# Attention backward loop on one core: result stores and operand loads issued piece by piece over the steps of a head group, and the PE-transposed blocks of dS copied out of PSUM in two pieces of 512 columns instead of four of 256

## The chip, the cores and the metric

The kernel runs on one core of one Trainium2 chip. The metric is device time in microseconds (us) of one execution. Before the change the median of three runs is 2866.06 us (2860.91 to 2873.49).

The core has a matrix engine (PE, with weight loads listed as PEld), a vector engine (DVE), an activation engine (ACT), a general engine (POOL) and a queue engine (SP) that here only issues DMAs. POOL also issues DMAs. All DMAs, whoever issues them, are moved by the same 16 DMA engines.

## The reference

The function is one transformer block with adaptive layer norm and its full backward pass (batch 1, 2048 tokens, width 512, 32 heads of 16, hidden width 1792). Cut to its core:

```python
def _A_ref(x, wqkv, wo):
    qkv = (x @ wqkv).reshape(B, S, 3, H, Dh) -> q, k, v      # H = 32, Dh = 16
    p = softmax(einsum('bhqd,bhkd->bhqk', q, k) * Dh ** -0.5)
    o = einsum('bhqk,bhkd->bhqd', p, v)
    return o.reshape(B, S, D) @ wo
...
h = layernorm(x) * (1 + ca) + sa;  x = x + ga * _A_ref(h, ...)
h = layernorm(x) * (1 + cb) + sb;  x = x + gb * (relu(h @ w1 + b1)**2 @ w2 + b2)
```

The outputs are the block's result and the gradients of x, wqkv, wo, w1, b1, w2, b2, c and w_mod for a given grad_out.

The change touches only the part that computes dQ, dK and dV of the attention. For each head, with E the unnormalised probabilities and dS = E * (dO V^T - delta): dV = E^T dO, dK = dS^T Q, dQ = dS K. The row constants and the 1/sum factors are folded into extra operand rows and pre-scaled operands, so the loop itself has only exponentials, one elementwise product and matmuls.

## The kernel before

The program first projects Q, K, V, runs the attention forward with the MLP forward and backward woven in as filler work (up to about 1300 us), then some weight gradients (the matmuls of line 800 and those before it), and then the backward loop of the attention (lines 813 to 963), which is what the change touches. A last stage turns dQ, dK, dV into the gradients of wqkv, x and the modulation.

**Tiling of the loop.** There are 8 head groups (`hg`) of 4 heads. A head group has 4 key chunks of 512 (`kc4`), each with 16 query tiles of 128 (`qt`), each with two head pairs (`pr`): 128 steps per head group, 1024 in all (`NS`). A step handles 2 heads x 128 queries x 512 keys, that is, a tile of 128 x 1024.

**A step's work.**
- `emit_S` (lines 823 to 833): PE writes the scores of two heads to a PSUM tile (`psS_u`, L829), ACT takes the exponential to SBUF (`E_u`, L833).
- `emit_D` (835 to 854): PE writes dO V^T - delta to a PSUM tile of the same pool (`psD_u`, L841), DVE multiplies it with `E_u` to `dS_u` (L847). `psS_u` and `psD_u` share three PSUM buffers (pool `psu`) in turn, so D of a step takes the buffer that S of the same step leaves when its exponential is done, and S of a step takes the buffer that D three steps earlier leaves when its product is done.
- `emit_V` (L883) and `emit_K` (L891): PE accumulates dV^T and dK^T in one PSUM bank, `accVK`, over the query tiles of a chunk.

**dQ.** It needs dS with keys on the partitions. Two steps (one query tile, four heads) make a `dS_u` tile of 16 blocks of 128 x 128; five such tiles are in use in turn. SP issues a transposing DMA for each (L853) into `dST`. Eight steps (four query tiles) make a group, 128 groups in all. Of the fourth tile of a group only 8 blocks go by DMA; the other 8 are transposed by PE (`emit_T`, L871, two halves of four blocks) into one PSUM bank (`dSt8`), and ACT copies them to `dST` (`emit_C`, L875, four copies of two blocks, 256 columns each). `emit_Q` (L912) then multiplies with K in three parts; ACT copies the result (`dQpart`, L923, or `dQacc`, L920 for the first chunk) and POOL adds it to `dQacc` (L925) or, in the last chunk, to the staged result `dQstage` (L930).

**Order of the work.** The main loop (936 to 963) emits, for step s: the next operand load if one is due, S of step s+1, D of s, V of s-1, K of s-2, and then by j = (s-10) mod 8: the transposes at j = 1 and 2, the copies at j = 1 to 4, the parts of Q at j = 5, 6, 7. All matmuls are chained in this order on PE, and all POOL work in its order on POOL. ACT's and DVE's order is set by the program's scheduler. ACT's order in a group, as it comes out, is: dQpart, two exponentials, copy, exponential, copy, copy, exponential, copy, four exponentials.

**Loads.** `load_one` brings an operand of the next head group: 16 loads of 17 rows x 2048 (68 KB) for `iq`, `ik`, `ido`, `iv`, and three of 512 KB for `sdo`, `sq`, `sk` (L744). They are issued on POOL's queue, one every 5 steps from step 32 of a head group. Each operand has two buffers, used by head groups in turn.

**Stores.** When a head group's dV^T and dK^T are staged in `dVKstage` (L898), `put_rows` (858 to 863) issues its 8 stores of 16 rows x 2048 (64 KB) at once; 4 more follow from `dQstage` about 8 steps later. In the last head group each chunk of 512 columns is stored as soon as it is staged.

**POOL's own order.** A step's number fixes only the place of a load or a store in POOL's order. POOL takes the next one when the one before is issued, unless it has to wait: an addition waits for ACT's copy of dQ, a load for the last reader of its buffer, and every DMA of POOL for the one eight DMAs earlier to have landed (eight semaphores are used in turn). Between two additions POOL therefore issues all that stands there. The first chunk of a head group has no additions, so everything that is put between the last `dQstage` addition (step 17) and the first `dQacc` addition (step 49 or later) stands in one piece. Before the change POOL's order around the start of a head group is: two additions to `dQstage`, each followed by a 512 KB load (`sq`, `sk`); the 8 stores of `dVKstage`; two additions; the 4 stores of `dQstage`; 4 loads of `iq`; then additions with one or two loads behind each.

Of the kernel before, what the change touches and what calls it, by code (L numbers as in the profile page):

```python
# [14 lines left out]
AF = mybir.ActivationFunctionType  # L15
ALU = mybir.AluOpType
AX = mybir.AxisListType
BF = dt.bfloat16
F32 = dt.float32

P = 128
# [3 lines left out]
DH = 16  # L25
HG = 8
# [7 lines left out]
def kernel(  # L34
# [8 lines left out]
    TT = n // P  # L43
    QC = n // 512
# [9 lines left out]
    ACT = nc.scalar  # L54
    POOL = nc.gpsimd
# [44 lines left out]
    qp_st = dram.tile([HG, P, TT, P], BF, name="qp_st")  # L100
    kp_st = dram.tile([HG, P, TT, P], BF, name="kp_st")
    dop_st = dram.tile([HG, P, TT, P], BF, name="dop_st")
# [7 lines left out]
    dT_st = dram.tile([3, D, n], BF, name="dT_st")  # L110
# [28 lines left out]
    with ExitStack() as ph:  # L139
# [5 lines left out]
        for ic in range(DC):  # L145
            pt = psA.tile([P, 8], BF, name="pst", tag="pst")
# [46 lines left out]
    with ExitStack() as ph:  # L193
# [36 lines left out]
        for t in range(TT):  # L230
            for which in range(3):
# [4 lines left out]
                if which < 2:  # L236
                    pad = tokpad[which][t % 2]
                    c0 = DH if which == 0 else 0
# [66 lines left out]
    with ExitStack() as ph:  # L305
# [19 lines left out]
        def chain(key, x):  # L325
            if key in last:
                issue_order(x, last[key])
            last[key] = x
# [405 lines left out]

    loads = {}
    LOADS = [(nm, src, j) for nm, src in (("iq", QtP), ("ik", KtP), ("ido", dOtP), ("iv", VtP)) for j in range(4)]
    LOADS += [("sdo", dop_st, None), ("sq", qp_st, None), ("sk", kp_st, None)]

    def load_one(hg, i):
        nm, src, j = LOADS[i]  # L740
        L = loads.setdefault(hg, {})
        if j is None:
            L[nm] = strm.tile([P, TT, P], BF, name=nm, tag=nm)
            chain("pool", POOL.dma_start(out=L[nm][:], in_=src[hg]))  # L744
        else:
            L[nm] = ops[nm][hg % 2]
            r = 32 * j
            chain("pool", POOL.dma_start(out=L[nm][r:r + DH + 1, :], in_=src[hg][r:r + DH + 1, :]))
# [63 lines left out]
    with ExitStack() as ph:  # L812
# [41 lines left out]
                             in_=dS_q[s // 2].rearrange("q h k -> q (h k)")[:, 0:nb * P], transpose=True)  # L854

        stage = {}

        def put_rows(st, hg, c0, w, parts):
            for t3, off in parts:
                for hq in range(4):  # L860
                    chain("pool", POOL.dma_start(
                        out=dT_st[t3, hg * 64 + hq * DH:hg * 64 + (hq + 1) * DH, c0:c0 + w],
                        in_=st[32 * hq + off:32 * hq + off + DH, c0:c0 + w]))

        def emit_T(g, half):
            if half == 0:
# [5 lines left out]

        def emit_C(g, j):
            pt = acc_t["T", g]
            ACT.activation(dST_t[g][:, 3, 8 + 2 * j:10 + 2 * j, :], pt[:, 2 * j:2 * j + 2, :], AF.Identity)  # L875
            if j == 3:
                del acc_t["T", g]

        def emit_V(s):
# [55 lines left out]

        emit_S(0)
        for s in range(NS + 12):
            r = s % (BLK * QC) - BLK
            if s < NS and r >= 0 and r % 5 == 0 and r // 5 < len(LOADS) and steps[s][0] + 1 < HG:
                load_one(steps[s][0] + 1, r // 5)  # L940
            if s + 1 < NS:
                emit_S(s + 1)
            if s < NS:
                emit_D(s)
            v = s - 1
            if 0 <= v < NS:
                if v % BLK == 0 and v > 0:
                    pass
                elif v % BLK == 1 and v > 1:
                    emit_V(v - 1)  # L950
                    emit_V(v)
                else:
                    emit_V(v)
            if 0 <= s - 2 < NS:
                emit_K(s - 2)
            g, j = divmod(s - GRP - 2, GRP)
            if 0 <= g < NS // GRP:
                if 1 <= j <= 2:
                    emit_T(g, j - 1)
                if 1 <= j <= 4:  # L960
                    emit_C(g, j - 1)
                for kt in ((0,), (1,), (2, 3))[j - 5] if j >= 5 else ():
                    emit_Q(g, kt)

# [153 lines left out]
```

## Time and profile before

| what | time |
|---|---|
| median of three runs | 2866.06 us |
| the profiled execution's own time | 2859.23 us |
| its span | 2857.4 us |
| first exponential of the backward loop to start of the last | 1367.7 to 2722.6 us |
| ACT busy / DVE busy / PE busy in the span | 2265.4 / 1844.6 / 2297.4 us |
| ACT exponentials of the loop, x1024 | 1030.4 us busy |
| DVE products of the loop, x1024 | 1216.8 us busy |
| ACT copies of dSt, x512 | 186.1 us busy, 392 ns mean |
| ACT copies dQpart | 597 ns median |
| 512 KB operand loads, issue to landing | 5.9 to 6.4 us median |
| 64 KB stores of dVKstage, issue to landing | 4.5 us median |
| transposing DMAs, issue to landing | 4.0 us median, 12.5 us at most |

Busy time of a group of instructions counts overlapping ones once. The instructions of ACT and DVE overlap at their ends: an exponential has a mean of 1034 ns, but two in a row start about 0.9 to 1.0 us apart. So a duration is not what an instruction costs in a chain; that is the distance from its start to the start of the next one that waits for nothing else. A row of the timeline has start, length, engine, line, what it writes and reads and the count; in brackets is the idle time of the engine before it and what ended that.

### The profile page before, as it was taken

To read this page: it belongs to the slowest core of one execution; us is meant where nothing else is said; L and a number is where in the kernel's file an instruction comes from. 1 tells how busy PE (TensorE), PEld (TensorE's weight loads), DVE (VectorE), ACT (ScalarE), POOL (GpSimd) and SP (SyncE) were. 2 spreads that over 40 slices of the span, in tenths; PEclk is the share of its full clock that TensorE was granted. 3 is DMA by queue.
4 is the path that set the end of the run, shared out by engine and by line. 5 is a ranking of instruction groups with operands and counts; after the bars stand their busy time and mean duration, and the time that the engine had idled before them with its cause. 6 is when DMAs were issued, how large, how long until landed. Compare 5 with 4: busy or idle time off the path is not lost.

```text
span 2857.4 us, 48379 instructions
## 1 busy us (share of the span) xinstructions
PE 2297.4 (80%) x18261; PEld 782.5 (27%) x18261; DVE 1844.6 (65%) x2376; ACT 2265.4 (79%) x2866; POOL 577.8 (20%) x766
## 2 busy tenths in 40 slices
PE   4888879778877976738888888888888888888868
PEld 2323223222322322314222222222222222222223
DVE  5533344424523442743798998989899898999944
ACT  3699999899989987010798998989899898999912
POOL 7311100410230041053012121111201112121221
PEclk8989969878986987878899999999999999999989
DMA  7931255534543554668699999999999999999985
GB/s 199 223 102 57 75 144 120 135 115 112 130 143 81 120 133 126 155 146 271 141 188 206 190 199 192 188 203 189 197 190 199 196 187 202 184 207 193 181 235 135
DMA packets 1275072, 470.60 MB, mean 165 GB/s; under 512 B 1219635, under 2 KB 1244342, under 8 KB 1273046
## 3 DMA queue, kind: packets, MB, share of 16 engines
q1 hardware_dynamic: 1239268, 357.49, 61.6%
q0 software_dynamic: 32704, 105.82, 12.4%
q10 hardware_dynamic: 2866, 4.20, 0.4%
q8 instruction: 144, 2.36, 0.4%
q14 instruction: 90, 0.74, 0.1%
HBM read 118.49 MB, written 72.56 MB: 67 GB/s over the span
## 4 chain that ended last, share of the span: by engine, by line
PE 16%; ACT 15%; DVE 15%; DMA 7%; issue 6%; SPq 1%; POOL 1%; DVEq 0%; ACTq 0%; POOLq 0%
DVE dS_u L847 13%; ACT E_u L833 12%; PE psD_u L841 4%; PE accVK L883 3%; DMA dST<-dS_u 3%; PE psS_u L829 3%; ACT dST L875 2%; PE dSt L871 2%; PE gb L800 1%; PE accQ L912 1%; DMA tT<-ac 1%; PE jb L1048 1%; DMA h2r<-xn_st 1%; DMA out_dram<-woblk 1%; DMA out_dram<-wqblk 1%
## 5 line engine op out<-in xcount | busy, mean ns | idle before, releaser
L847 DVE TENSOR_TENSOR dS_u<-psD_u,E_u 128x1024 bf16<-128x1024 f32 x1024 | 1216.8, 1220 | 142.8 <-PE psD_u L841 92.1
L833 ACT ACTIVATE E_u<-psS_u 128x1024 bf16<-128x1024 f32 x1024 | 1030.4, 1034 | 80.3 <-PE psS_u L829 56.5
L606 ACT ACTIVATE ET<-sbank 128x1024 bf16<-128x1024 f32 x1024 | 948.6, 1111 | 52.8 <-PE sbank L603 50.9
L841 PE MATMUL psD_u<-iv,ido 32*128 32x512 bf16 x2048 | 412.7, 393 | 170.8 <-ACT E_u L833 155.7
L829 PE MATMUL psS_u<-ik,iq 32*128 32x512 bf16 x2048 | 410.6, 397 | 24.6 <-DVE dS_u L847 18.8
L891 PE MATMUL accVK<-dS_u,sq 128*32 128x512 bf16 x2048 | 415.7, 402 | 0.5 <-DVE dS_u L847 0.5
L883 PE MATMUL accVK<-E_u,sdo 128*32 128x512 bf16 x2048 | 403.8, 403 | 0.0
L603 PE MATMUL sbank<-qt_sb,kt_sb 32*128 32x512 bf16 x2048 | 229.7, 434 | 88.7 <-ACT ET L606 73.3
L613 PE MATMUL oacc<-ET,va 128*32 128x512 bf16 x2048 | 233.7, 445 | 57.3 <-ACT ET L606 54.9
L841 PEld LDWEIGHTS <-ido 32*128 32x128 bf16 x2048 | 164.0, 91 | 357.3 <-issue 355.5
L925 POOL TENSOR_TENSOR dQacc<-dQpart,dQacc 128x512 f32<-128x512 f32 x64 | 80.8, 1262 | 870.9 <-ACT dQpart L923 870.9
L875 ACT ACTIVATE dST<-dSt 128x256 bf16<-128x256 bf16 x512 | 186.1, 392 | 30.5 <-PE dSt L871 30.0
L912 PE MATMUL accQ<-dST,sk 128*32 128x512 bf16 x2048 | 189.9, 392 | 1.2 <-ACT dST L875 1.0
L829 PEld LDWEIGHTS <-iq 32*128 32x128 bf16 x2048 | 102.1, 91 | 320.4 <-issue 294.8
L883 PEld LDWEIGHTS <-sdo 128*32 128x32 bf16 x2048 | 97.4, 93 | 237.8 <-issue 237.8
L603 PEld LDWEIGHTS <-kt_sb 32*128 32x128 bf16 x2048 | 80.8, 93 | 226.1 <-issue 213.0
L613 PEld LDWEIGHTS <-va 128*32 128x32 bf16 x2048 | 66.4, 95 | 257.7 <-issue 257.7
L710 ACT ACTIVATE dwmod_sb<-dmodbc,silucol 128x2048 bf16<-128x2048 bf16 (+1 forms) x8 | 11.9, 1563 | 131.1 <-DVE dmodbc L689 131.1
L275 PE MATMUL xb<-h1T,wpadT 128*128 128x512 bf16 x364 | 99.6, 398 | 15.6 <-DVE pst L574 8.8
L619 DVE COPY ostage<-oacc 128x512 f32<-128x512 f32 x32 | 22.0, 688 | 131.9 <-PE oacc L613 131.9
L871 PE MATMUL dSt<-identb,dS_u 128*128 128x128 bf16 x1024 | 104.4, 226 | 1.2 <-ACT dQpart L923 0.7
L891 PEld LDWEIGHTS <-sq 128*32 128x32 bf16 x2048 | 99.1, 93 | 8.6 <-issue 8.5
(232 smaller groups left out, 2346.4 us busy)
## 6 DMA issues: line engine op xcount, KB each, us to landing
wbig<-in_B_w_dram POOLq DMA_DIRECT2D x8, 1792.0 KB, 9.4
kt_sb<-KtP SPq DMA_DIRECT2D x24, 512.0 KB, 3.7
va<-va_st SPq DMA_DIRECT2D x32, 336.0 KB, 4.3
dST<-dS_u SPq DMA_TRANSPOSE x512, 4.0
wbig<-w2T_st POOLq DMA_DIRECT2D x4, 1792.0 KB, 13.1
wbig<-w1T_st POOLq DMA_DIRECT2D x4, 1792.0 KB, 8.6
dztok_st<-tokh POOLq DMA_DIRECT2D x8, 896.0 KB, 4.8
dzq<-dztok_st SPq DMA_DIRECT2D x4, 1792.0 KB, 26.4
```

The lines of the kernel that those rows point to most:

```text
L603: pe(PE.matmul(pair_ps[hq // 2][:, hq % 2, :], kt_sb[r:r + 32, kt * P:(kt + 1) * P], qt_sb[r:r + 32, :], start=True, stop=True, tile_posit ...
L606: ACT.activation(ET_t[u][:, 2 * pair:2 * pair + 2, :], pair_ps[pair][:], AF.Exp, scale=SCALE)
L613: pe(PE.matmul(oacc[32 * hq:32 * hq + 32, :], lhsT, ET_t[u][:, hq, :], start=(kt == 0), stop=(kt == TT - 1), tile_position=(0, 32 * hq), s ...
L829: pe(PE.matmul(ps[:, hi, :], L["iq"][r:r + 32, qt * P:(qt + 1) * P], L["ik"][r:r + 32, kc4 * 512:(kc4 + 1) * 512], start=True, stop=True, ...
L833: ACT.activation(E_t[s][:], ps[:], AF.Exp, scale=SCALE)
L841: pe(PE.matmul(ps[:, hi, :], L["ido"][r:r + 32, qt * P:(qt + 1) * P], L["iv"][r:r + 32, kc4 * 512:(kc4 + 1) * 512], start=True, stop=True, ...
L847: DVE.tensor_tensor(dS_t[s], ps[:], E_t[s][:], ALU.mult)
L871: pe(PE.transpose(pt[:, j, :], src[:, (8 + j) * P:(9 + j) * P], identb[:]))
L875: ACT.activation(dST_t[g][:, 3, 8 + 2 * j:10 + 2 * j, :], pt[:, 2 * j:2 * j + 2, :], AF.Identity)
L883: pe(PE.matmul(accVK[r:r + 32, :], loads[hg]["sdo"][:, qt, r:r + 32], E_t[s][:, hi, :], start=(qt == 0), stop=False, tile_position=(0, r), ...
L891: pe(PE.matmul(accVK[r:r + 32, :], loads[hg]["sq"][:, qt, r:r + 32], dS_t[s][:, hi, :], start=False, stop=(qt == TT - 1), tile_position=(0 ...
L912: pe(PE.matmul(accQ[r:r + 32, :], L["sk"][:, kc4 * 4 + kt, r:r + 32], dST_t[g][:, :, hq * 4 + kt, :], start=(kt == 0), stop=(kt == 3), til ...
```

## The change

Three things change in the backward loop; PE's, DVE's and SP's instructions and their order stay as they are.

- The three 512 KB loads are each cut into four of 128 KB (128 rows x 512 instead of 128 x 2048). With the 16 others that makes 28 loads per head group, issued one every 3 steps from step 22 (to step 103) instead of 19, one every 5 steps from step 32 (to step 122).
- The stores of a head group are put on a list and issued one at a time, at every fourth step, from step 5 of the next head group (the 8 of dVKstage) to step 49 (the 4 of dQstage). In the last head group everything on the list is issued at once, as before. POOL's order around the start of a head group becomes: three additions to `dQstage`, 2 stores of `dVKstage`, the fourth addition, then 20 DMAs with nothing between them (the other 6 stores of `dVKstage`, the 4 of `dQstage`, and 10 loads: 4 `iq`, 4 `ik`, 2 `ido`), then additions with two or three loads behind each.
- The PE-transposed blocks are copied by ACT in two pieces of 512 columns, at j = 2 and 3, instead of four of 256 at j = 1 to 4. ACT's order in a group becomes: dQpart, three exponentials, copy, exponential, copy, four exponentials.

```diff
-    LOADS += [("sdo", dop_st, None), ("sq", qp_st, None), ("sk", kp_st, None)]
+    LOADS += [(nm, src, 4 + j) for nm, src in (("sdo", dop_st), ("sq", qp_st), ("sk", kp_st)) for j in range(4)]
...
-        if j is None:
-            L[nm] = strm.tile([P, TT, P], BF, name=nm, tag=nm)
-            chain("pool", POOL.dma_start(out=L[nm][:], in_=src[hg]))
+        if j >= 4:
+            if j == 4:
+                L[nm] = strm.tile([P, TT, P], BF, name=nm, tag=nm)
+            ts = slice((j - 4) * TT // 4, (j - 3) * TT // 4)
+            chain("pool", POOL.dma_start(out=L[nm][:, ts, :], in_=src[hg][:, ts, :]))
...
+        rows = []
+
+        def put_row():
+            st, hg, c0, w, t3, off, hq = rows.pop(0)
+            chain("pool", POOL.dma_start(
+                out=dT_st[t3, hg * 64 + hq * DH:hg * 64 + (hq + 1) * DH, c0:c0 + w],
+                in_=st[32 * hq + off:32 * hq + off + DH, c0:c0 + w]))
 
         def put_rows(st, hg, c0, w, parts):
             for t3, off in parts:
                 for hq in range(4):
-                    chain("pool", POOL.dma_start(
-                        out=dT_st[t3, hg * 64 + hq * DH:hg * 64 + (hq + 1) * DH, c0:c0 + w],
-                        in_=st[32 * hq + off:32 * hq + off + DH, c0:c0 + w]))
+                    rows.append((st, hg, c0, w, t3, off, hq))
+            while hg == HG - 1 and rows:
+                put_row()
...
-            ACT.activation(dST_t[g][:, 3, 8 + 2 * j:10 + 2 * j, :], pt[:, 2 * j:2 * j + 2, :], AF.Identity)
-            if j == 3:
+            ACT.activation(dST_t[g][:, 3, 8 + 4 * j:12 + 4 * j, :], pt[:, 4 * j:4 * j + 4, :], AF.Identity)
+            if j == 1:
...
-            r = s % (BLK * QC) - BLK
-            if s < NS and r >= 0 and r % 5 == 0 and r // 5 < len(LOADS) and steps[s][0] + 1 < HG:
-                load_one(steps[s][0] + 1, r // 5)
+            r = s % (BLK * QC) - 22
+            if s < NS and r >= 0 and r % 3 == 0 and r // 3 < len(LOADS) and steps[s][0] + 1 < HG:
+                load_one(steps[s][0] + 1, r // 3)
+            if rows and s % 4 == 1:
+                put_row()
...
-                if 1 <= j <= 4:
-                    emit_C(g, j - 1)
+                if 2 <= j <= 3:
+                    emit_C(g, j - 2)
```

## The prediction

> **What bounds the kernel now.** I read the page first (shares and slices), then the spans of each stage, the waits inside the backward loop, and then the timeline of one undisturbed group, engine by engine, because the shares do not settle it:
>
> ```profile
> L833 ACT ACTIVATE E_u<-psS_u x1024: 1016/1024/1072, 1367.7 to 2722.6; 128x1024 bf16<-128x1024 f32 x171
> ...
> 1537.00:1707.00 170.00, 146.02 (x1424) 45.53 (x1420) 152.80 (x129) 152.62 (x213) 30.24 (x43) 0.97 1.03 198
> ```
>
> The first line (the tile view of E_u) puts the loop between 1367.7 and 2722.6: 1354.9 us for 1023 steps. The second (busy time by stretch; PE, PEld, DVE, ACT, POOL, then granted clock, DMA share, GB/s) is one head group: DVE 152.80 and ACT 152.62 of 170, PE 146.02. Nothing is full. So the loop runs on a chain that crosses engines. One group on ACT:
>
> ```profile
> 1645.81 0.60 ACT L923 ACTIVATE dQpart<-accQ 128x512 f32<-128x512 f32 x1 [0.35 <-PE accQ L912]
> 1646.30 1.94 ACT L833 ACTIVATE E_u<-psS_u 128x1024 bf16<-128x1024 f32 x2
> 1648.46 0.38 ACT L875 ACTIVATE dST<-dSt 128x256 bf16<-128x256 bf16 x1 [0.22 <-PE dSt L871]
> 1648.79 1.02 ACT L833 ACTIVATE E_u<-psS_u 128x1024 bf16<-128x1024 f32 x1
> 1649.71 0.66 ACT L875 ACTIVATE dST<-dSt 128x256 bf16<-128x256 bf16 x2
> 1650.23 1.04 ACT L833 ACTIVATE E_u<-psS_u 128x1024 bf16<-128x1024 f32 x1
> 1651.14 0.42 ACT L875 ACTIVATE dST<-dSt 128x256 bf16<-128x256 bf16 x1
> 1651.40 2.04 ACT L833 ACTIVATE E_u<-psS_u 128x1024 bf16<-128x1024 f32 x2
> 1653.82 1.99 ACT L833 ACTIVATE E_u<-psS_u 128x1024 bf16<-128x1024 f32 x2 [0.39 <-PE psS_u L829]
> 1656.16 0.60 ACT L923 ACTIVATE dQpart<-accQ 128x512 f32<-128x512 f32 x1 [0.35 <-PE accQ L912]
> ```
>
> and the part of PE's that matters:
>
> ```profile
> 1647.37 0.39 PE L841 MATMUL psD_u<-iv,ido 32*128 32x512 bf16 x2 [0.66 <-ACT E_u L833]
> ...
> 1648.03 0.40 PE L871 MATMUL dSt<-identb,dS_u 128*128 128x128 bf16 x4
> 1648.36 0.39 PE L829 MATMUL psS_u<-ik,iq 32*128 32x512 bf16 x2
> ...
> 1653.39 0.39 PE L829 MATMUL psS_u<-ik,iq 32*128 32x512 bf16 x2
> ```
>
> From dQpart to dQpart a group takes 10.35 us. Undisturbed, 1023 steps would take 1023 x 10.35 / 8 = 1323.5; the loop loses 1354.9 - 1323.5 = 31.4 us to stalls. They sit where the 512 KB loads and the stores are:
>
> ```profile
> DVE dS_u L847 <- DMA dST<-dS_u: 19.9, 13, 4.2
> ```
>
> ```profile
> 1700.43 0.56 POOL L744 DMA_DIRECT2D sk<-kp_st  x1
> 1709.34 3.86 POOL L861 DMA_DIRECT2D dT_st<-dVKstage  x8 [8.35 <-ACT dVKstage L898]
> ...
> 1721.53 1.95 POOL L861 DMA_DIRECT2D dT_st<-dQstage  x4 [0.30 <-POOL dQstage L930]
> 1723.47 1.99 POOL L748 DMA_DIRECT2D iq<-QtP  x4
> ```
>
> ```profile
> 1718.57 6.99 DVE L847 TENSOR_TENSOR dS_u<-psD_u,E_u 128x1024 bf16<-128x1024 f32 x6 [1.20 <-DMA dST<-dS_u]
> ...
> 1730.42 4.72 DVE L847 TENSOR_TENSOR dS_u<-psD_u,E_u 128x1024 bf16<-128x1024 f32 x4 [2.20 <-DMA dST<-dS_u]
> ```
>
> ```profile
> 1730.10:1743.80 13.70, 11.93 (x90) 3.34 (x90) 11.50 (x10) 9.77 (x13) 0.00 (x0) 0.63 1.04 201
> ```
>
> DVE waits for a dS_u buffer whose transposing DMA is late (13 times, 19.9 us), and after such a wait the granted clock is 0.63 and the group takes 13.70 instead of 10.35.
>
> **Part 1, the copies.** Removed per group: four copies of 256 columns. Added: two of 512. The first row to look at is the exponential at 1648.79. It starts 0.43 after its S at 1648.36; the one at 1653.82, which waits for PE by the profile, also starts 0.43 after its S (1653.39). So it is PE that sets 1648.79: the chain is exponential end, D at 1647.37, transposes at 1648.03, S at 1648.36. The copy at 1648.46 fills a hole, and taking it out gains nothing. Then ACT runs without a pause to 1651.40: exponential, two copies (1649.71 to 1650.23, 0.52), exponential (0.91), copy (1651.14 to 1651.40, 0.26). That stretch holds three old copies, 0.78 us, and will hold both new ones.
>
> What one new copy takes in it no row shows. From below: the start-to-start of a 256 copy (0.26) and of a 1024 exponential (0.91) give 0.65/768 = 0.85 ns a column, so 512 columns take 0.26 + 0.22 = 0.48. Nearest row: dQpart, 512 columns, 1645.81 to 1646.30, 0.49. From above: its whole length 0.60, if nothing overlapped. I take 0.48: 2 x 0.48 - 0.78 = **+0.18 us a group** (upper end +0.42). The exponential at 1651.40 starts 0.18 later, and D, V, Q and S at 1653.39 follow it in PE's order, so the group ends 0.18 later. Some 15 of 128 groups are disturbed by stalls and would hide it; 113 x 0.18 = **+20 us** (0.165 at the least, +19; with 0.42, +47). A gain is not excluded by this alone; it is the second rival.
>
> One page reads the same rows otherwise. ACT's page share in the loop equals DVE's, and the Trainium skill ("Perfetto Trace Analysis", Optimizing Scalar/DVE Operations) says that a Scalar operation pays about 51 ns of access on PSUM and that grouping helps if the engine is saturated; two operations fewer would by it be -0.10 a group, -13 us over 128. The trace agrees on the size (0.26 less 0.22 for the columns is 0.04) and not on the condition: ACT stands idle before 1648.46, 1653.82 and 1656.16.
>
> The transposes' halves (1648.43 and some 1649.4) end 1.3 us and more before the new copies' places, and the shared PSUM bank is read out by about 1651.7, before Q needs it at 1653.07: no new wait. PE, DVE and SP keep their orders.
>
> **Part 2, stores and loads.** What can go is the 31.4. What is the new pattern? The three 512 KB loads become 128 KB ones, two or three behind each addition, 10 us apart: 0.3 MB per group where sq and sk brought 0.5 MB each. They are finished by step 103, so the last three groups of a head group carry none; before, sk lies right ahead of the stores. I take those stalls as gone. But POOL is not held to the steps: behind the last dQstage addition (1719.96 in the trace) 20 DMAs of 64 or 68 KB stand in one piece where 8 stood (1721.53 and 1723.47). At 0.49 us an issue and at most eight in flight (landing 4.5 us in the median) they take 10 to 15 us and bring 1.3 MB. Before, 2.1 MB fell into the 41 us from sq to iq. So one burst stays, longer than each of the old ones but with nothing ahead of it. How late does it make the transposes? The old burst of 8 stores (3.86 us) moved one transpose's landing from 4.0 to about 7.0 us; a dS_u tile may be late by four tiles of 2.6 us, 10.4 us from issue, before DVE stalls. A burst 2 to 3 times as long adds 6 to 9 us: 10 to 13 us, at the edge. I put 1.5 to 2 us of stall, clock drop included, at each of 7 boundaries, 12 us. So 31 - 12 = **-19 us**. Ends: all gone, -31; the burst as bad as all before, 0, or, with 20 DMAs for 8, another 10 us on top.
>
> The other queues: 9 more DMA issues per head group and 9 ahead of the loop, 72 in all x 0.56 us = 40 us of POOL. It is covered by POOL's waiting for dQpart (870.9 us at L925); a dQ addition can be late by 3 x 0.56 = 1.7 us and its buffer is needed two groups, 20 us, later. Loads start 10 steps earlier, and the last reader of their buffer is at step 9, ahead of 22. SP issues what it did. In the last head group 4 leftover stores join the first 8 (2 us on POOL, no reader until after the loop). The tail's stores come as before.
>
> **Sum.** Against the profiled execution: 2859.2 + 20 - 19 = 2860. It was faster than all three timed runs (2860.91 to 2873.49); the median is 6.8 above it, and I carry half: 2860 + 3.4, say **2863**. No change, then, by the bound of 0.5% (14 us), about what a measurement of this kernel can tell from none.
>
> **Rivals.**
> - *Forecast: the copies cost what the stores return*, 2863. Its own range is 2852 to 2878. Chance 0.50.
> - *The burst takes the place of the old stalls.* 20 DMAs in one piece, eight in flight throughout, hold the transposes up beyond the 10.4 us. For it: two bursts of 8 with 8 us between them already gave 1.20 and 2.20 us of waiting and a clock of 0.63. Against: nothing precedes it now. From a stall of 4.5 us a boundary on (7 x 4.5 = 31) nothing is returned: 2866 + 20 = 2886, slower; with 10 more, 2896. Chance 0.25.
> - *ACT is the bound after all*, and less ACT time is a shorter group: copies' start-to-start was 0.33 + 0.52 + 0.26 = 1.11, becomes 0.96, -0.15 x 128 = -19, with stalls -19: 2863 - 20 - 19 = 2824. For it: ACT is as busy as DVE. Against: the 0.43 above. Chance 0.07. (The page named above would have it; its own figure, -13, gives 2830.)
> - *All stalls go*, as the diff has it: 2859.2 + 19 - 31 = 2847, and since slow runs then lose their excess too I add nothing. Chance 0.18.
>
> **Numbers.** Faster by over 0.5% is below 2851.7: ACT's 0.07, two thirds of the last (0.12), a little of the forecast: 0.21. Slower is above 2880.4: most of the second, 0.24. The same: 0.55. The range leaves out the ACT case and the upper part of the burst: 2842 to 2888.
>
> **What would show it.** Copies: groups of 10.5 instead of 10.35 between dQparts; ACT's waits for psS_u (56.5 us) up by some 60, as the hole at 1648.24 is empty; none for dSt. If groups are 10.2, ACT was the bound. Stalls: DVE's waits for dST's transposes below 10 us and no clock of 0.63 between head groups; if they remain, they should sit 15 to 35 us behind a head group's start, at POOL's 20 DMAs in one piece. A new copy of other than 0.60 us, or a burst that POOL does not issue in one piece, would make me wrong.

## The result, and the profile after

The change takes 2882.65 us in the median (2872.67 to 2891.29 over 20 runs), the kernel before, on the same chips, 2868.93 (2860.91 to 2880.82): a ratio of 1.0035, 95% interval 1.0023 to 1.0048, slower by 0.35%. The forecast was 2863, range 2842 to 2888, and "the same" within 0.5%. The time lies in the range and in the bound of 0.5%. But the forecast stood 0.2% under this median of the kernel before (0.1% under the 2866.06 known then), and the measurement 0.35% above it: the small difference has the other sign.

The profiled execution of the change took 2879.92 us (span 2878.1), 20.7 more than that of before. That is more than the 13.7 between the medians: the profiled execution of before lay 9.7 under its median, that of the change 2.7. So the following shows where time goes, and exaggerates the loss by some 7 us. In the tile view of the exponentials (shortest, middle and longest duration in ns, then first and last start):

```profile
L835 ACT ACTIVATE E_u<-psS_u x1024: 1017/1025/1068, 1363.2 to 2747.1; 128x1024 bf16<-128x1024 f32 x171
```

The backward loop now lasts 2747.1 - 1363.2 = 1383.9 us instead of 1354.9: +29.0. It began 4.5 us earlier and 3.8 us are gained behind it; the loop's start lies between 1363 and 1376 in the runs below, whatever the kernel, so these two say nothing about the change. The busy time of the loop by stretch (stretch, length, then PE, PEld, DVE, ACT and POOL in us, granted clock, DMA share, GB/s), before and after:

```profile
1367.70:2722.60 1354.90, 1163.75 (x11202) 362.81 (x11201) 1214.33 (x1022) 1215.21 (x1689) 237.90 (x339) 0.96 1.00 192
```

```profile
1363.20:2747.10 1383.90, 1169.42 (x11203) 356.14 (x11202) 1219.39 (x1022) 1182.06 (x1435) 269.56 (x396) 0.95 0.96 188
```

ACT has 33 us less to do and the loop takes 29 us more. Three readings divide the 29.

**The undisturbed group.** ACT's timeline of one group after the change (start, us, engine, operation, how many in a row, and in brackets the idle time before with what ended it), and the S matmuls of PE that belong to it:

```profile
1594.85 0.60 ACT L929 ACTIVATE dQacc<-accQ 128x512 f32<-128x512 f32 x1 [0.40 <-PE accQ L921]
1595.35 1.93 ACT L835 ACTIVATE E_u<-psS_u 128x1024 bf16<-128x1024 f32 x2
1597.83 1.02 ACT L835 ACTIVATE E_u<-psS_u 128x1024 bf16<-128x1024 f32 x1 [0.55 <-PE psD_u L843]
1598.75 0.59 ACT L884 ACTIVATE dST<-dSt 128x512 bf16<-128x512 bf16 x1
1599.22 1.03 ACT L835 ACTIVATE E_u<-psS_u 128x1024 bf16<-128x1024 f32 x1
1600.13 0.62 ACT L884 ACTIVATE dST<-dSt 128x512 bf16<-128x512 bf16 x1
1600.61 1.97 ACT L835 ACTIVATE E_u<-psS_u 128x1024 bf16<-128x1024 f32 x2
```

```profile
1597.40 0.39 PE L831 MATMUL psS_u<-ik,iq 32*128 32x512 bf16 x2
...
1602.58 0.39 PE L831 MATMUL psS_u<-ik,iq 32*128 32x512 bf16 x2
```

The exponential at 1597.83 still starts 0.43 behind its S at 1597.40. The place where the first small copy stood is now 0.55 us of idle ACT. The two copies take 1598.75 to 1599.22 and 1600.13 to 1600.61, 0.47 and 0.48 start to start, and what follows them on ACT starts that much later. In the median a group takes 10.495 us instead of 10.355: 0.14 x 128 = 17.9 us.

**The half-clock windows.** In a group at full clock (first line) and in one with a half-clock window (second line), and in the window itself (third):

```profile
1474.69:1485.19 10.50, 8.74 (x92) 2.72 (x88) 9.30 (x9) 9.12 (x11) 2.83 (x4) 1.00 1.06 214
1463.24:1474.69 11.45, 9.93 (x92) 2.83 (x88) 9.92 (x9) 9.23 (x11) 2.30 (x3) 0.85 0.97 213
1470.70:1474.10 3.40, 3.40 (x32) 0.76 (x28) 2.83 (x3) 2.05 (x3) 0.00 (x0) 0.50 1.02 229
```

For 3.4 us the clock is 0.50, PE is busy throughout, and the group takes 11.45 instead of 10.50: 0.95 us. Such windows begin always at the same place, 7.3 to 7.7 us after the start of a group's copy of accQ (dQpart or dQacc), 14 times in the loop. Two of the 14 belong to stalls between head groups (1566.27, and 2088.51, which lasts 13.65 us). The other 12 are single windows inside a head group, at least 14 us from any wait of DVE for a DMA. Before the change there were 4, at 7.35 to 7.4. Eight more at 0.95 are 7.6 us.

**The stalls between head groups.** What is left of the loop is 1383.9 - 1342.0 (1023 steps at 10.495 / 8) - 12 x 0.95 = 30.5 us; before it was 1354.9 - 1324.1 - 4 x 0.95 = 27.0. So in this pair of executions the stalls, from which the prediction took 19 us, are all still there. The waits of DVE and POOL (waiting tile, what it waited for, then us in total, times, longest):

```profile
DVE dS_u L849 <- DMA dST<-dS_u: 15.8, 7, 4.7
...
POOL dT_st L863 <- DMA iq<-QtP: 12.8, 5, 3.2
```

Seven waits of DVE, at five of the 7 boundaries between head groups, have taken the place of 13 (19.9 us before). At a sixth boundary PE waits 1.6 us for a transposing DMA instead, and the last has no stall. POOL's timeline at one boundary, and DVE's behind it:

```profile
1548.88 1.25 POOL L939 TENSOR_TENSOR dQstage<-dQpart,dQacc 128x512 bf16<-128x512 f32 x1 [8.29 <-ACT dQpart L932]
1550.09 1.49 POOL L863 DMA_DIRECT2D dT_st<-dVKstage  x3
1551.56 1.01 POOL L750 DMA_DIRECT2D iq<-QtP  x2
...
1559.87 0.50 POOL L863 DMA_DIRECT2D dT_st<-dQstage  x1 [3.18 <-DMA iq<-QtP]
...
1565.39 0.50 POOL L863 DMA_DIRECT2D dT_st<-dQstage  x1
1605.97 1.26 POOL L934 TENSOR_TENSOR dQacc<-dQpart,dQacc 128x512 f32<-128x512 f32 x1 [40.09 <-ACT dQpart L932]
```

```profile
1565.07 2.36 DVE L849 TENSOR_TENSOR dS_u<-psD_u,E_u 128x1024 bf16<-128x1024 f32 x2 [0.67 <-DMA dST<-dS_u]
1570.19 4.63 DVE L849 TENSOR_TENSOR dS_u<-psD_u,E_u 128x1024 bf16<-128x1024 f32 x4 [2.76 <-ACT E_u L835]
```

```profile
1570.30:1584.40 14.10, 12.53 (x90) 3.39 (x90) 11.83 (x10) 10.12 (x13) 0.00 (x0) 0.64 1.00 199
```

From 1550.09 to 1565.89 POOL issues the 20 DMAs that the program puts at steps 13 to 49, and then waits 40 us for its next addition. DVE waits for a transposing DMA at the end of the burst and once more, for ACT, behind it, and the next group (last fence, by stretch) runs at a clock of 0.64 and takes 14.10 us.

### The profile page after: what moved, and what is told of

Same layout as the page of the kernel before. It is cut to its first block, busy times and chain, and to the rows that moved or that the text cites. A ratio compares the mean times of both kernels' runs of the same rounds, so it can differ in the third digit from the quotient of the medians.

```text
span 2878.1 us, 48099 instructions
## 1 busy us (share of the span) xinstructions
PE 2287.2 (79%) x18153; PEld 775.5 (27%) x18261; DVE 1851.3 (64%) x2376; ACT 2232.9 (78%) x2610; POOL 618.0 (21%) x838
## 4 chain that ended last, share of the span: by engine, by line
PE 16%; ACT 15%; DVE 12%; issue 9%; DMA 7%; SPq 1%; POOL 0%; ACTq 0%; DVEq 0%; another core or an unknown queue 0%; POOLq 0%
ACT E_u L835 12%; DVE dS_u L849 10%; PE psD_u L843 4%; PE accVK L892 3%; PE psS_u L831 3%; DMA dST<-dS_u 3%; ACT dST L884 3%; PE dSt L880 2%; PE accQ L921 1%; PE gb L802 1%; DMA tT<-ac 1%; PE jb L1059 1%; DMA h2r<-xn_st 1%; DMA out_dram<-woblk 1%; DMA out_dram<-wqblk 1%
## 5 line engine op out<-in xcount | busy, mean ns | idle before, releaser
L835 ACT ACTIVATE E_u<-psS_u 128x1024 bf16<-128x1024 f32 x1024 | 1015.2, 1033 | 166.0 <-PE psD_u L843 153.5
L843 PEld LDWEIGHTS <-ido 32*128 32x128 bf16 x2048 | 158.0, 91 | 383.0 <-issue 380.9
L921 PE MATMUL accQ<-dST,sk 128*32 128x512 bf16 x2048 | 196.2, 403 | 4.9 <-DMA dST<-dS_u 3.6
L884 ACT ACTIVATE dST<-dSt 128x512 bf16<-128x512 bf16 x256 | 154.3, 603 | 1.2 <-PE dSt L880 0.7
```

Source lines behind the costliest of these rows:

```text
L835: ACT.activation(E_t[s][:], ps[:], AF.Exp, scale=SCALE)
L843: pe(PE.matmul(ps[:, hi, :], L["ido"][r:r + 32, qt * P:(qt + 1) * P], L["iv"][r:r + 32, kc4 * 512:(kc4 + 1) * 512], start=True, stop=True, ...
L884: ACT.activation(dST_t[g][:, 3, 8 + 4 * j:12 + 4 * j, :], pt[:, 4 * j:4 * j + 4, :], AF.Identity)
L921: pe(PE.matmul(accQ[r:r + 32, :], L["sk"][:, kc4 * 4 + kt, r:r + 32], dST_t[g][:, :, hq * 4 + kt, :], start=(kt == 0), stop=(kt == 3), til ...
```

## The experiments

The theory with which I began: the copies cost what they were said to cost, and the burst makes the stalls, since POOL, which nothing holds back, carries out 40 us of the program at once. Rivals: the stalls are due to the amount of data and not to its bunching; ACT's time is what counts; the windows of half clock are chance. "At that place" below means half-clock windows that begin 6.9 to 7.7 us after the start of the group's copy of accQ. Windows and groups (the median length) are counted in the one profiled execution of each kernel. Ratios are to the kernel before, with 95% intervals; the kernel before was measured again beside each batch of runs (medians 2865.72 to 2873.30), so runs of different batches are compared by their ratios. The added matmuls write a tile that the following S overwrites, and the added POOL copy writes a tile that nobody reads.

### One half of the change at a time

The kernel before with the two copies alone:

```diff
-            ACT.activation(dST_t[g][:, 3, 8 + 2 * j:10 + 2 * j, :], pt[:, 2 * j:2 * j + 2, :], AF.Identity)
-            if j == 3:
+            ACT.activation(dST_t[g][:, 3, 8 + 4 * j:12 + 4 * j, :], pt[:, 4 * j:4 * j + 4, :], AF.Identity)
+            if j == 1:
...
-                if 1 <= j <= 4:
-                    emit_C(g, j - 1)
+                if 2 <= j <= 3:
+                    emit_C(g, j - 2)
```

> Only the copies are changed: two of 512 columns at j = 2 and 3 instead of four of 256; loads and stores as before. Theory A (the copies are the loss: each group is longer because both copies stand on ACT's chain, and the longer stretch in which PE mostly waits lets the clock gate take away half the clock for one 3.41 us window more often): groups of 10.50 us instead of 10.35 (+18 us over 128), single half-clock windows inside a head group up from about 4 to about 13 (0.95 us each, +8), stalls between head groups as before (about 26 us): 20 to 28 us slower than before, ratio 1.007 to 1.010. Theory B (the new pattern of loads and stores is the loss, the copies are neutral as in a stretch with slack): groups of 10.35, within 4 us of before.

Measured: 2894.04, ratio 1.0070 (1.0039 to 1.0100); group 10.497, 12 windows at that place.

The change with the four copies of 256 columns kept (the same diff backwards):

> Only the loads and stores are changed; the four copies of 256 columns stay. Theory A: groups of 10.35 us and few half-clock windows as before; POOL issues 20 DMAs in one piece behind the last addition to dQstage, and the stall moves from the end of a head group to its second and third group without getting smaller: 25 to 30 us of it, within 6 us of before. Theory B: 15 to 25 us slower than before. Theory C (the stores and loads are spread as the step numbers say): stalls nearly gone, 20 to 28 us faster.

Measured: 2862.14, ratio 0.9970 (0.9952 to 0.9987); group 10.355, 6 windows. DVE's waits for the transposing DMAs, with the copies alone and with the spreading alone:

```profile
DVE dS_u L847 <- DMA dST<-dS_u: 27.8, 14, 5.8
```

```profile
DVE dS_u L849 <- DMA dST<-dS_u: 16.5, 7, 5.2
```

What follows: the parts add up (+0.70 - 0.30 = +0.40%, measured +0.35%). The copies cost 20 us (0.70% of 2868.93; by the interval 11 to 29). The spreading returns 9 (0.30%; 4 to 14) and not 19. The 7 waits belong to the spreading.

### POOL held to the steps

A copy of one column that needs a fresh `dQacc` makes POOL wait in each of the first four groups of a head group, so that what the program puts behind it isn't issued before. It is added to the spreading alone:

```diff
+        pace = stg.tile([P, 1], F32, name="pace", bufs=1)
...
+                    chain("pool", POOL.tensor_copy(pace[:, 0:1], dQacc[:, qc * 512:qc * 512 + 1]))
```

> As the run with loads and stores alone, plus one small POOL copy per group of the first key chunk (128x1, reads what ACT has just written to dQacc), so that POOL waits for every group and issues 4 or 5 DMAs per 10 us there instead of 20 in one piece. Theory A (the burst makes the stall): stalls between head groups fall from 26 to 29 us to under 8, no half-clock windows longer than 3.41 us between head groups: 18 to 25 us faster than before. Rival (the amount of bytes in the first 40 us of a head group makes it, not the burst): as the run with loads and stores alone.

Measured: 2833.33, ratio 0.9875 (0.9850 to 0.9900). POOL's timeline behind the same additions:

```profile
1565.07 0.18 POOL L931 COPY pace<-dQacc 128x1 f32<-128x1 f32 x1 [8.06 <-ACT dQacc L930]
1565.29 0.48 POOL L864 DMA_DIRECT2D dT_st<-dVKstage  x1
1565.78 1.01 POOL L750 DMA_DIRECT2D iq<-QtP  x2
1566.78 0.50 POOL L864 DMA_DIRECT2D dT_st<-dVKstage  x1
1575.41 0.18 POOL L931 COPY pace<-dQacc 128x1 f32<-128x1 f32 x1 [8.13 <-ACT dQacc L930]
```

Four DMAs, then 8 us of waiting: no wait of DVE for a transposing DMA is left anywhere in the loop, which by stretch is

```profile
1372.10:2702.00 1329.90, 1145.27 (x11202) 357.74 (x11201) 1214.72 (x1022) 1211.66 (x1689) 279.71 (x438) 0.98 1.00 196
```

The loads and stores are those of the spreading alone, in number and size, only later. So the bunching makes the stalls, not the data: 2862.14 - 2833.33 = 29 us. Against the kernel before it is 1.25%, 36 us, more than the 18 to 25 that were expected. The same line added to the whole change:

> The whole change, plus the small POOL copy per group that makes POOL wait in the first key chunk. Theory A: the burst's stalls (29 us in the profile of the change) go to under 4 us, the copies' cost stays (groups 10.50 us, 12 to 14 half-clock windows at 0.95 us): 22 to 29 us faster than the change, 26 us slower than the paced run with the old copies: 2854 to 2862 us, 8 to 15 us faster than before. Rival (the copies' loss is bound up with the burst): 2833 to 2840 us.

Measured: 2854.54, ratio 0.9960 (0.9946 to 0.9974); group 10.494, 12 windows, no wait of DVE for a DMA. By the ratios the pace is worth 0.75% here, 21 us (0.95%, 27 us, on the spreading alone), and the copies cost 0.85%, 24 us, against the paced spreading (0.70% without the pace). Within the intervals the two halves are independent.

### The copies put into the hole

If the copies cost what they cost by their place, they should gain when they stand where ACT waits for PE. The kernel before with transposes and copies one step earlier, the copies at j = 1 and 2:

```diff
-                if 1 <= j <= 2:
-                    emit_T(g, j - 1)
-                if 1 <= j <= 4:
-                    emit_C(g, j - 1)
+                if 0 <= j <= 1:
+                    emit_T(g, j)
+                if 1 <= j <= 2:
+                    emit_C(g, j - 1)
```

> Two copies of 512 columns, but the PE transposes are put one step earlier (j = 0 and 1) and the copies too (j = 1 and 2), so that the first copy falls into ACT's idle time before the third exponential; loads and stores as before. Theory A (a group is a chain over PE and ACT, and only what is on it counts): between the third and the fifth exponential stands one copy of 0.48 us instead of 0.78 us of copies: groups of 10.0 to 10.1 us, 30 to 42 us faster than before less what half-clock windows take or give. Rival (ACT's or DVE's total work sets the group): DVE's 9.5 us are unchanged and ACT's work falls by 0.15, so 10.2 at best.

Measured: 2879.79, ratio 1.0039 (1.0012 to 1.0067). The undisturbed group is 10.18, shorter than the 10.355 of before by 0.175 (the expectation said 10.0 to 10.1), and yet the loop does not gain. Two stretches of it, the loop and one run of seven groups:

```profile
1369.20:2730.50 1361.30, 1208.41 (x11200) 379.14 (x11200) 1203.23 (x1022) 1207.77 (x1435) 238.75 (x339) 0.94 1.00 191
...
1402.60:1475.00 72.40, 66.52 (x564) 18.56 (x564) 61.31 (x51) 59.49 (x72) 6.18 (x8) 0.79 0.80 165
```

DVE's waits for DMAs are down to 2.1 us, but the granted clock is 0.94 over the loop, and 0.79 over seven groups on end: 30 stretches at half clock in the whole loop, one in each group for a while. Half-clock stretches last whole multiples of 3.41 us, and in each run that has them their starts lie on one grid of that step. Three steps are 10.24, close to this group's 10.18, so once a window of the clock falls on the wrong place, it falls close to it again in the next groups. With the windows, a shorter group is no faster kernel. The place of the copies is worth 0.3 us a group (10.495 to 10.18), and something else is taking the clock.

With the paced spreading added:

> Paced loads and stores together with the early transposes and the two early copies. Groups of 10.18 us are close to three clock windows (3 x 3.41 = 10.24), so the group drifts slowly past the windows and half-clock windows come in rows of five and more, as in the run with early copies alone: 20 to 30 of them at 0.9 us, no stall between head groups. Theory A: 2835 to 2845 us, no faster than the paced run with the old copies, although each undisturbed group is 0.17 us shorter. Rival (the rows of half-clock windows were set off by the stalls at the loads and stores): 2810 to 2818 us.

Measured: 2846.43 (2824.66 to 2860.7), ratio 0.9915 (0.9886 to 0.9945); group 10.18, 35 half-clock stretches in the loop (12 of them at that place), loop 1351.0 at a clock of 0.93. That is just above the 2835 to 2845 expected, and far from the rival's 2810 to 2818: the rows of windows come without any stall, and the kernel is slower than the paced spreading with the old copies, whose group is longer.

### What takes the clock inside a group

The windows begin at one place, so they follow on one stretch: with windows of 3.41 us, the stretch from 4.0 us to 7.4 us after the start of the copy of accQ, which is steps j = 3 to 5, where ACT has both copies and PE waits for ACT. PE waits in it twice, 0.36 and 0.37 us; in the 3.41 us before the window at 1470.70 it is busy for 2.68. The first attempt was to keep PE busy there, by S written twice at j = 3 and 4:

```diff
-            for hi in range(2):
+            for hi in (0, 1, 0, 1) if (s - 11) % GRP in (3, 4) else (0, 1):
```

> The run with the copies alone, and PE does the S matmuls of two steps a group twice (j = 3 and 4, same result into the same PSUM tile), in time in which it waits for ACT. Theory A (single half-clock windows come because PE does too little in the stretch of the two copies): single windows of 3.41 us inside head groups fall from 14 to at most 4, groups stay at 10.50 us, 8 to 12 us faster than the run with the copies alone. Rival (the windows come from something else, an instruction fetch or the DMAs): as many windows as before, and the same time or a little more.

Measured, on the copies alone: 2898.44, ratio 1.0117 (1.0092 to 1.0142); 16 windows at that place, 7.19 to 7.41, and four more at 8.4 to 8.5. At most 4 were expected, and the refutation is not conclusive: the order on ACT had changed as well, and the two copies stood next to each other.

> The run with paced loads and stores and the four old copies, with the same two S matmuls done twice. Theory A: the 5 single half-clock windows of the paced run go, 4 to 5 us faster than it (2828 to 2830 us). Rival (the filling costs PE time on the chain): the groups grow above 10.35 us and it is slower than the paced run.

Measured, on the paced spreading: 2833.74, ratio 0.9882 (0.9863 to 0.9902), the same as without, where 4 to 5 us were expected; 4 windows instead of 5, here too with copies moved together.

> As the run before it, with the two S matmuls done twice. Theory A (too little PE work in the stretch is what takes the clock away): hardly any half-clock windows, groups of 10.18 us throughout: 128 x 0.17 = 22 us below the paced run with old copies and its 5 windows: 2805 to 2815 us. Rival: no better than without the filling.

Measured, on the early copies: 2815.48, ratio 0.9813 (0.9790 to 0.9835), the fastest kernel of all, 31 us less than without the fill; 2 windows in the loop instead of 35:

```profile
1371.00:2722.00 1351.00, 1211.42 (x11208) 377.68 (x11207) 1205.18 (x1023) 1208.57 (x1435) 279.88 (x438) 0.93 0.99 193
```

```profile
1363.10:2680.20 1317.10, 1226.86 (x11712) 384.68 (x11712) 1194.83 (x1022) 1211.65 (x1435) 279.84 (x438) 0.99 1.03 198
```

The first line is the loop with early copies and pace, the second the same with S twice: 510 matmuls more on PE, 34 us less. But the group is 10.22 here, nearer to three windows and drifting otherwise, so the fill and the drift are not told apart by this run alone. The fill at three steps (j = 3, 4, 5):

> Paced loads and stores, early transposes and copies, S twice at j = 3, 4 and 5. The run with j = 3 and 4 had 2 half-clock windows left inside the loop. Theory A: nothing left to gain there, the third extra pair stands on PE ahead of a D that no longer waits: 0 to 5 us slower than 2815. Rival (more PE work still helps): below 2810.

Measured: 2828.79, ratio 0.9862 (0.9841 to 0.9884), 2 windows; but 30 groups took 10.68, and by the ratios the kernel is 14 us slower than with two fills, where 0 to 5 were expected. That the third fill stands on PE's chain is my reading, and no run shows it.

Back to the copies alone, filled where ACT's order stays as it was (j = 4 and 5, `in (4, 5)` in the same line):

> The copies alone, and S done twice at j = 4 and 5 instead of 3 and 4. In the run with j = 3 and 4 the scheduler also put ACT's two copies next to each other, so it did not tell the causes apart; here ACT's order is that of the run with the copies alone. The half-clock windows there begin 7.4 to 7.6 us behind a dQpart, that is, they follow the 3.41 us from 4.0 on, in which PE does only the steps j = 3 to 5; both extra pairs fall into it. Theory A (too little PE work in these 3.41 us): the windows at 7.4 to 7.6 us, 14 in the run with the copies alone, fall to at most 3 and the groups stay within 0.1 us of 10.50: 8 to 12 us faster than that run. Rival (they are not due to PE's work there): about as many, and the same time.

Measured: 2881.93, ratio 1.0056 (1.0039 to 1.0073); 10 windows, now at 7.09 to 7.28. At most 3 were expected, so that PE's busy time sets it is refuted in this form. S uses 32 rows of weights. So the last form of the theory was that it is not the time that counts but how much of the array is used: one matmul with 128 x 128 weights over 512 columns ahead of S at j = 4 and 5:

```diff
+            for hi in range(1 if (s - 11) % GRP in (4, 5) else 0):
+                pe(PE.matmul(ps[:, hi, :], identb[:], L["ik"][:, kc4 * 512:(kc4 + 1) * 512], start=True, stop=True))
```

> The copies alone, and ahead of the S matmuls at j = 4 and 5 one matmul of 128 x 128 weights by 512 columns into the same PSUM tile, which S then overwrites (the result does not change). S done twice there used a quarter of PE's rows and took the windows from 14 to 10 and from 7.45 to 7.2 us behind dQpart. Theory A (the clock gate counts PE's work in these 3.41 us): a matmul over the whole array counts for more, so at most 4 windows of 3.41 us inside head groups, 6 to 10 us faster than the copies alone. Rival (it does not count PE's work): 10 or more windows.

Measured: 2873.32, ratio 1.0002 (0.9986 to 1.0018), by the ratios 0.68% or 19.5 us less than the copies alone (6 to 10 were expected), and **no** window at that place. Six are left, all behind stalls. PE's timeline at the place:

```profile
1487.80 0.39 PE L843 MATMUL psD_u<-iv,ido 32*128 32x512 bf16 x2
...
1488.45 0.39 PE L828 MATMUL psS_u<-ik,identb 128*128 128x512 bf16 x1
1488.77 0.39 PE L831 MATMUL psS_u<-ik,iq 32*128 32x512 bf16 x2
1489.20 0.39 PE L843 MATMUL psD_u<-iv,ido 32*128 32x512 bf16 x2
```

```profile
1368.90:2757.30 1388.40, 1168.38 (x11202) 356.92 (x11201) 1218.80 (x1022) 1182.86 (x1435) 237.88 (x339) 0.95 0.97 188
```

```profile
1373.30:2735.90 1362.60, 1243.37 (x11457) 386.56 (x11456) 1216.11 (x1022) 1206.33 (x1434) 237.84 (x339) 0.98 0.99 191
```

The added matmul at 1488.45 stands in the 0.36 us for which PE waited anyway. Second and third fence: the loop with the copies alone, and with the two added matmuls. 255 matmuls more, the group in the median as long as before (10.50, though 26 groups take 10.62), and the clock up from 0.95 to 0.98. Twelve windows at 0.95 us are 11 us of the gain; for the rest, the stretches at half clock behind the stalls are shorter too (6.83 us at most, where up to 13.65 were). Twice as many (two at each place):

> The same with two such matmuls at each of the two places (0.43 us of PE, more than the 0.36 us that PE waits there). Theory A: no windows of 3.41 us inside head groups; groups up to 0.15 us longer than 10.50, which takes the gain back: 0 to 10 us faster than the copies alone. Rival: as many windows as with one, and 10 to 20 us slower for the longer groups.

Measured: 2883.85, ratio 1.0049 (1.0028 to 1.0070); no window at that place either, but 28 groups take 10.84: two no longer fit into the wait. And on the early copies with pace, one at j = 3 and 4:

> Paced loads and stores, early transposes and copies, and one full-array matmul ahead of S at j = 3 and 4, where PE waits 0.48 and 0.36 us in the run with early copies. Theory A: no half-clock windows inside head groups, groups of 10.18 to 10.22 us: 2808 to 2815 us, as with S done twice there (2815) or a little better, about 55 us faster than before. Rival (the 10.18 us groups were only lucky against the clock windows when S was done twice): windows come back in rows and it takes 2830 us or more.

Measured: 2822.62, ratio 0.9854 (0.9832 to 0.9875); no window, loop clock 1.00, group 10.327:

```profile
1366.20:2690.00 1323.80, 1241.94 (x11462) 387.29 (x11461) 1201.83 (x1022) 1219.02 (x1435) 279.84 (x438) 1.00 1.02 197
```

The group is far from 10.22, so it is not the drift of the filled version alone that frees a kernel of windows. But the time is above the 2808 to 2815 expected, for the group grows by 0.15 us, and that is paid in each. Without the fill PE waits 0.48 and 0.36 us there, so the matmuls have room; why the group grows even so stays open.

**The array in use, in all traces.** The sixteen traces hold more than these pairs of runs. Take every step of the 3.41 us grid that ran at full clock, from 45 us behind the first exponential of the loop to 10 us before the last, 5797 in all, and add up the matmuls in it: each counts by the part of the 128 x 128 array that its weights cover and by its columns, so that the added matmul of `copies_full45` counts 1 and one S matmul (32 rows) 0.25. Of the 5554 steps with a sum of 6.0 or more, none was followed by half clock; of the 145 with less than 5.6, 142 were; between the two, 56 of 98. PE's busy time does not divide them so: it reached 2.99 us in steps that were followed by half clock, and was under 3.0 in 2586 that were not.

In undisturbed groups the sum is lowest in a stretch that ends 6.6 to 7.2 us behind the copy of accQ: 4.8 before the change, 4.6 with the copies alone, 5.6 with S twice at j = 4 and 5, and 6.6 with the full matmul. With the early copies and the pace it is 4.7, with S twice 5.6, with one full matmul 6.2. So S twice lifts both kernels by about 1.0, to the edge, and the full matmul lifts them past it.

The number of windows then hangs on the length of the group too. Against three steps of the grid a group of 10.355 us moves by 0.115 each time and one of 10.495 by 0.255, so the grid passes the low place about twice as often. In the paced kernels, which have no stalls, the windows are 24 groups apart with the old copies (5 in the loop) and 10 apart with the new (12). The low place was there before the change; the copies made it a little lower and, above all, let it be met more often.

## Why the prediction was wrong, step by step

**The copies (+20): right in the chain.** 0.48 us start to start was taken, 0.47 and 0.48 were measured; the exponential at j = 3 still hangs on its S by 0.43; the group went to 10.495 ("10.5 instead of 10.35"), 17.9 us over the loop. That the copies alone cost 20 us as a whole kernel is in part luck, for their extra windows, which no term had, are in it too. ACT's waits for PE ahead of exponentials rose as said, though they are now put down mostly to D (153.5) and no longer to S (11.1): together 165 against 78, up by 87 where "some 60" was said. The rival "ACT is the bound after all" is out: 33 us less of ACT, and a longer loop. The Trainium skill ("Perfetto Trace Analysis", Optimizing Scalar/DVE Operations) gives the access time of an operation, from which the prediction estimated 13 us less for two operations fewer a group; it says that grouping can help if the engine is saturated, and that condition is what this case lacked. The runs show the other side too: moved to where ACT stands idle, the same two copies shorten the group by 0.3 us.

**The stalls, "31 − 12 = −19": this is the step that failed.** The run with the spreading alone returned 9 us (4 to 14) and not 19, which is the size of the miss between the forecast and the measured +0.35%, 10 us. In the profiled pair it looks worse: loop less undisturbed groups, the 30.8 (31.4 with the prediction's 10.35) became 41.9, +11 instead of -19. The step had two errors of different kinds.
- *The stall at a boundary.* "1.5 to 2 us … clock drop included" was taken; it was (41.9 - 12 x 0.95) / 7 = 4.4 us in the mean. The working had everything in it: the 20 DMAs in one piece, 10 to 15 us of them (15.8 measured), a lateness of "10 to 13 us, at the edge" of the 10.4 at which DVE stalls. I took the lower edge. DVE's waits for the DMAs are 2.3 us a boundary (15.8 / 7), and the low clock in the group behind them (0.64 in the one shown) adds to that. They sit 28 to 39 us behind a head group's start, at the end of the burst; "15 to 35 us" was said. This is the mechanism of the rival that the burst takes the place of the old stalls: "from a stall of 4.5 us a boundary on nothing is returned", 2886, measured 2882.65. As a difference it said +20 where the ratio gives +10, for the spreading did return something; its time is near by luck. It had a chance of 0.25 and deserved more.
- *The half-clock windows.* The 31.4 held 4 of them inside head groups, which the prediction took for DMA stalls. The copies raised them to 12: +7.6 us that no term had. The trace of before shows them, in a list of group lengths, as groups longer by 0.95 us; the prediction went by the clock of one head group as a whole (0.97).

What the runs show and what is only argued: that the burst makes the stalls is shown (same data, paced: 21 and 27 us less by the ratios, no wait left). That copies and spreading are independent is shown within the noise (0.40 against 0.35%; 20 and 24 us for the copies, unpaced and paced). That the windows depend on what PE does in its waiting time behind ACT's copies is shown (12 to 0 by 255 matmuls, 19.5 us). That it goes by the part of the array in use, rather than by busy time, is borne out by one pair of runs (S twice, 12 to 10; full array, 12 to 0) and by the count over all traces; the bound of 5.6 to 6.0 is that of this kernel's matmuls, and a few per cent of matmul records may be missing. Why the fill with S did so well on the early copies (35 to 2) when it did little here has a likely answer in the same count: both fills reach only the edge (5.6), but a group of 10.22 moves by 0.02 against the grid and meets the low place hardly at all, one of 10.50 by 0.26. That share of the drift was not tested by a run of its own.

**The rest.** The nine more DMA issues and the loads' earlier start cost nothing that shows, as said. Half of the 6.8 us between the profiled execution and the median was carried; the medians differ by 13.7, the profiled executions by 20.7, and the start of the loop alone moves by 13 us from run to run: at this size one profiled execution is no basis for the last 5 us.

## What to carry to other kernels

A step number in a program paces nothing on an engine that has nothing to wait for. If transfers are to be spread, a cheap instruction that depends on the step (0.18 us on POOL here) must stand between them; that was worth 21 to 29 us, where the spreading without it returned 9.

A copy is priced by its place: in a hole of its engine it is free, behind the chain's last input it costs its whole start-to-start time, whatever the engine's share of busy time. Before two engines' programs are rearranged for less busy time, look at which wait ends last at each place.

List the granted clock period by period. A loop whose mean clock is 0.95 can be losing 1 us in one group of ten at a fixed place, and a stretch in which PE is thin but never idle for long is enough.

## What the runs showed of the hardware

- The clock is taken with PE far from idle. After the change the window of half clock at 1470.70 follows 3.41 us in which PE is busy for 2.68 and waits 0.37 us at most at one time. The Trainium skill ("TensorE: Matmul & The Clock Gate", HAM oscillation — how this bites in real kernels) warns of idle gaps above about 3.4 us. The windows' length and clock agree (3.40 us here, at 0.50); the condition doesn't: the longest wait in the stretch, 0.37 us, is about a ninth of that.
- Whether work keeps the clock goes with the part of the array that it uses: matmuls with 32 rows of weights, two more at each of two steps, left 10 of 12 windows; one of 128 x 128 at each left none. Over all traces the clock was kept behind every 3.41 us with a sum of 6.0 or more (in matmuls of 128 x 128 by 512), and lost behind 142 of 145 with less than 5.6. With one matmul in each wait of 0.36 us the median group was as long as before; with two, 28 groups took 10.84 us instead of 10.50.
- A loop whose period is near a multiple of the window (10.18 against 10.24 us) falls into step with it and loses the window again and again: about 30 times, a clock of 0.79 over seven groups, enough to cancel a group shorter by 0.175 us. It takes a low place as well: with S twice (5.6 instead of 4.7) and a group of 10.22, two windows were left.
- The best kernel of the study has all that it teaches: copies in the hole, paced spreading, and PE's wait filled. 2815.48 us, 1.9% under the kernel before.
